# Pooled attention with a two-layer block behind it: the first batch's weight tiles are transposed on TensorE and multiplied by V in float32, and GpSimd rounds the high halves of the layer weights

## The chip, the core and the metric

The kernel runs on one core of one Trainium2 chip. The core has TensorE (PE; its weight loads are listed apart as PEld), VectorE (DVE), ScalarE (ACT), GpSimd (POOL) and SyncE (SP, which here only issues DMAs), each with its own instruction queue that runs in order. SBUF holds tiles of 128 partitions; TensorE writes to PSUM, from which ScalarE and VectorE read. The metric is the device time of one execution in microseconds (us). Every time below is from one profiled execution or from the timed runs that are named.

## The reference

Attention with pooled queries, then layer normalisation, two matrix products with a ReLU between them, and a residual:

```python
# q, k, v: (4, 8, 1152, 64) float32
q_pool = q.reshape(B, H, S // 2, 2, D).mean(axis=3)          # 576 query rows
scores = (1 / sqrt(D)) * q_pool @ k.transpose(0, 1, 3, 2)     # 576 x 1152 per head
attn = exp(scores - max(scores))
attn = attn / (sum(attn) + 1e-09)
x = attn @ v                                                 # to (4, 576, 512)
xn = (x - mean(x)) / sqrt(var(x) + 1e-06) * g_ln
out = x + relu(xn @ w_ch1) @ w_ch2                           # 512 -> 2048 -> 512
```

All inputs and the output are float32.

## The kernel before

**Precision.** Matrix products run on float16 pairs: each float32 operand is scaled by a power of two and split into a high half and a low half (what the high half left over), and three products are summed: high by high, high by low, low by high. `split_from` (L258) makes such a pair from PSUM: ScalarE writes the high half (L261), VectorE the low one (L262).

**Steps.** Two heads of one batch make a pair; there are 16 pairs of 9 steps each, 144 steps in all. A step handles one tile of 128 query rows against 1152 keys. Steps 0 to 35 are the first batch. In each pair the fifth tile (j = 4) holds the last 64 rows of both heads. `step(i)` (L850) records the work of a step in a fixed order, by hand, and each engine runs its share in that order:

- `emit_max(i)`: VectorE finds each row's maximum in PSUM (L334) and the exponent's offset (L335);
- if tile i-1 is transposed on TensorE, ScalarE and VectorE take its transpose out of PSUM (L261 and L262, tile pt);
- `emit_s(i + 1)`: nine score matmuls (L321; eighteen where j = 4) into the slot of PSUM that tile i-1 had. There are two slots, so these matmuls wait until tile i-1 has left its slot;
- `flush`: results that wait in PSUM are taken out (division by the row sums L432, L435, L439, the splits of K and Q);
- `emit_exp(i)`: ScalarE's exponential, out of PSUM into the float32 tile pe (L340);
- `a_piece`: the product of one earlier tile with V (`emit_pv`, L399);
- `some_units`: one preparation of the next pair's K or Q (six per pair, transposes L272, L275, L286) and one unit of the layer block (L520, L551), if one is ready;
- `emit_t(i)`: nine transposes of pe (L373), into the slot that the scores of tile i held;
- what was put down for this step: loads, bounds of K, Q and V by an absolute sum on ScalarE (L179), splits of V and of the layer weights.

**Two ways to transpose.** The weights of a tile must have keys on the partitions before they are multiplied by V. `on_pe` (L297) decides how. On TensorE (20 of the first batch's 36 tiles): the nine transposes, then four passes that split them out of PSUM. By DMA (the other 16, and all 108 tiles of the other batches): ScalarE writes the high half (L354), GpSimd (L238, L361) or VectorE (L363) the low half, and SP issues a DMA transpose (L366). In the first batch the low half of these is always GpSimd's. Either way `emit_pv` does 27 matmuls of 64 or 65 columns (54 half-wide ones where j = 4). The 65th column of V is one, so that it gives the row sum.

**V.** `split_v` (L240) makes V's pair on GpSimd in three passes for each head (L238 twice, L256), with a scale from the bound of V; for the first pair ScalarE and VectorE do it.

**Layer weights.** 32 blocks of 512 KB are loaded through staging buffers (L613), ScalarE takes their absolute value (L618) and VectorE rearranges their bits in three passes (L106); then 16 tiles are scaled on GpSimd (L238), rounded to the high half on ScalarE (L695), and GpSimd subtracts (L699). These are put down by step number: the blocks in steps 1 to 24 and 24 to 47, the splits after each quarter. The layer block starts at step 41, when the first batch's rows are complete. From there one of its 144 units goes with each step, and what is left runs after the last step.

## Time and profile before

| | us |
|---|---|
| three timed runs | 1001.45, 1002.28, 1005.26 (median 1002.28) |
| profiled execution | 1000.85 |
| its span, first to last instruction | 999.0 |

| engine | busy us | share of the span | instructions |
|---|---|---|---|
| PE | 841.4 | 84% | 9505 |
| PEld | 580.7 | 58% | 9505 |
| DVE | 674.9 | 68% | 1208 |
| ACT | 570.3 | 57% | 789 |
| POOL | 394.7 | 40% | 341 |

The share of an engine over the whole span is a mean over stages with different limits. The span is therefore read stage by stage: the first batch (from the first row maximum to that of step 36), the next steps, the long stretch to the last step, and the units left over. Beside the busy time stands the clock that TensorE was granted: 1.0 is 2.4 GHz, 0.5 is 1.2 GHz, and a number between is a stretch that had both.

### The profile page before, as it was taken

What the parts mean: (1) busy time and instruction counts of PE and PEld (TensorE: products, weight loads), DVE (VectorE), ACT (ScalarE), POOL (GpSimd) and SP (SyncE); (2) the same over time, 40 slices, a digit from 0 to 9 for tenths busy, and PEclk for the clock granted to TensorE, in tenths of its full rate; (3) what the DMA queues carried; (4) which work ended last, traced back from release to release, by engine and by line L of the source; (5) the groups of instructions that cost most, each with busy time, mean ns of one, the idle gap of its engine ahead of it and who ended that gap; (6) DMA issues with size and microseconds to landing.
All of it is one profiled execution on the core that took longest, in us unless ns stands there. A gap on an engine that the chain in (4) does not pass through costs nothing.

```text
span 999.0 us, 22406 instructions
## 1 busy us (share of the span) xinstructions
PE 841.4 (84%) x9505; PEld 580.7 (58%) x9505; DVE 674.9 (68%) x1208; ACT 570.3 (57%) x789; POOL 394.7 (40%) x341
## 2 busy tenths in 40 slices
PE   6565586666766679999969899999989999999998
PEld 4354464545545447666647567576656757767665
DVE  5496587867897787876777777677766777652211
ACT  3666366655655556866767577677676766521000
POOL 2253255744644455845362525344443232310000
PEclk7597676756767899999999999999998999999999
DMA  4456445463464865879787888979696867710000
GB/s 119 110 114 154 117 96 157 97 163 97 103 162 82 187 136 102 161 157 189 156 154 150 144 167 142 182 137 180 102 195 119 168 134 134 132 27 12 1 22 22
DMA packets 309044, 124.40 MB, mean 125 GB/s; under 512 B 292304, under 2 KB 292304, under 8 KB 308944
## 3 DMA queue, kind: packets, MB, share of 16 engines
q1 hardware_dynamic: 308592, 122.09, 59.8%
q8 instruction: 74, 1.21, 0.5%
q10 hardware_dynamic: 352, 0.88, 0.3%
q14 instruction: 26, 0.21, 0.1%
HBM read 45.09 MB, written 4.72 MB: 50 GB/s over the span
## 4 chain that ended last, share of the span: by engine, by line
PE 46%; DVE 29%; ACT 7%; DMA 5%; POOL 5%; issue 5%; SPq 3%; ACTq 0%; POOLq 0%; DVEq 0%
PE psum L520 15%; PE psum L551 13%; PE psum L399 7%; PE psum L321 7%; DVE mx L334 7%; DVE stage L106 4%; DVE hl L363 3%; DVE pt L262 2%; SPq L366 2%; DMA vr<-in_v_dram 2%; DVE ht L534 2%; ACT pe L340 1%; DVE wsl L106 1%; ACT kt L261 1%; DVE kt L262 1%
## 5 line engine op out<-in xcount | busy, mean ns | idle before, releaser
L321 PE MATMUL psum<-kt,qt 64*128 64x512 f16 (+3 forms) x1440 | 175.3, 363 | 63.2 <-DVE pt L262 51.5
L334 DVE TENSOR_REDUCE mx<-psum 128x1 f32<-128x1152 f32 x144 | 194.2, 1349 | 49.8 <-PE psum L399 45.7
L340 ACT ACTIVATE pe<-psum,nb,sc 128x1152 f32<-128x1152 f32 x144 | 188.7, 1310 | 25.5 <-DVE nb L335 24.6
L551 PE MATMUL psum<-wsl,ht 128*128 128x512 f16 x864 | 198.7, 383 | 2.2 <-DVE qt L262 2.0
L520 PEld LDWEIGHTS <-wsl 128*128 128x128 f16 x1920 | 174.0, 100 | 29.5 <-issue 6.2
L520 PE MATMUL psum<-xn,wsl 128*128 128x256 f16 x1536 | 183.3, 279 | 5.4 <-DVE kt L262 3.3
L399 PE MATMUL psum<-vt,pt 128*128 128x65 f16 (+3 forms) x4320 | 173.4, 201 | 0.0
L399 PEld LDWEIGHTS <-pt 128*128 128x128 f16 (+1 forms) x4320 | 157.7, 106 | 26.8 <-issue 25.2
L321 PEld LDWEIGHTS <-qt 64*128 64x128 f16 (+1 forms) x1440 | 74.0, 104 | 149.6 <-issue 115.8
L439 ACT ACTIVATE xb<-psum,r 128x64 f32<-128x64 f32 x128 | 39.9, 312 | 203.0 <-DVE r L435 196.2
L354 ACT ACTIVATE hl<-pe 128x1152 f16<-128x1152 f32 x124 | 144.3, 1164 | 13.2 <-DMA pt<-hl 9.5
L238 POOL TENSOR_SCALAR pe<-pe 128x1152 f32<-128x1152 f32 x52 | 60.7, 1168 | 208.6 <-ACT hl L354 198.3
L551 PEld LDWEIGHTS <-ht 128*128 128x128 f16 x864 | 82.4, 98 | 94.0 <-issue 6.0
L361 POOL TENSOR_TENSOR hl<-pe,hl 128x1152 f16<-128x1152 f32 x52 | 123.9, 2383 | 4.3
L363 DVE SCALAR_TENSOR_TENSOR hl<-pe,hl 128x1152 f16<-128x1152 f32 x72 | 107.9, 1498 | 0.0
L533 ACT ACTIVATE ht<-psum 128x512 f16<-128x512 f32 x72 | 42.7, 594 | 94.5 <-PE psum L520 94.2
L534 DVE SCALAR_TENSOR_TENSOR ht<-psum,ht 128x512 f16<-128x512 f32 x72 | 49.6, 689 | 69.7 <-ACT ht L533 69.0
L238 POOL TENSOR_SCALAR vt<-vr,s 128x576 f16<-128x576 f32 x30 | 23.6, 786 | 94.4 <-DVE s L231 94.4
L262 DVE SCALAR_TENSOR_TENSOR kt<-psum,s,kt 128x512 f16<-128x512 f32 (+1 forms) x48 | 31.5, 657 | 40.3 <-ACT kt L261 40.3
L161 POOL TENSOR_TENSOR qr<-qr 128x1152 f32<-128x1152 f32 (+1 forms) x8 | 21.7, 2714 | 88.1 <-DMA qr<-in_q_dram 71.0
L262 DVE SCALAR_TENSOR_TENSOR qt<-psum,s,qt 128x384 f16<-128x384 f32 x48 | 29.5, 615 | 36.4 <-ACT qt L261 36.4
L373 PE MATMUL psum<-ident,pe 128*128 128x128 f32 x180 | 33.9, 353 | 18.5 <-ACT pe L340 18.4
(104 smaller groups left out, 899.0 us busy)
## 6 DMA issues: line engine op xcount, KB each, us to landing
stage<-in_moe_w_ch_dram SPq DMA_DIRECT2D x32, 512.0 KB, 4.7
kr<-in_k_dram SPq DMA_DIRECT2D x16, 576.0 KB, 4.3
qr<-in_q_dram SPq DMA_DIRECT2D x31, 288.0 KB, 6.0
vr<-in_v_dram SPq DMA_DIRECT2D x15, 576.0 KB, 4.9
out_dram<-xb SPq DMA_DIRECT2D x32, 128.0 KB, 2.5
pt<-hl SPq DMA_TRANSPOSE x124, 4.7
vr<-in_v_dram ACTq DMA_DIRECT2D x1, 576.0 KB, 6.2
out_dram<-xh SPq DMA_DIRECT2D x4, 128.0 KB, 3.4
```

Source lines behind the costliest of these rows:

```text
L238: nc.gpsimd.tensor_scalar(dst, src, s, 1.0, op0=ALU.mult, op1=ALU.mult)
L262: lambda: nc.vector.scalar_tensor_tensor(lo, ps, s, hi, op0=ALU.mult, op1=ALU.subtract),
L321: nc.tensor.matmul(out=sp[o:o + w, c0:c0 + n], lhsT=qt[r:r + 64, qa, q0:q0 + w], rhs=kt[r:r + 64, ka, h, k0:k0 + n], start=(a == 0), stop= ...
L334: nc.vector.tensor_reduce(mx, st["s"], axis=AX.X, op=ALU.max)
L340: nc.scalar.activation(out=st["pe"], in_=st["s"], func=ACTF.Exp, scale=pair[i // C]["sc"][:, 0:1], bias=st["nb"],)
L354: nc.scalar.activation(out=hl[:, 0], in_=st["pe"], func=ACTF.Copy, scale=2.0 ** 15)
L361: nc.gpsimd.tensor_tensor(hl[:, 1], st["pe"], hl[:, 0], op=ALU.subtract)
L363: nc.vector.scalar_tensor_tensor(hl[:, 1], st["pe"], 2.0 ** 15, hl[:, 0], op0=ALU.mult, op1=ALU.subtract)
L399: nc.tensor.matmul(out=dst[:, 0:n], lhsT=lhsT, rhs=rhs, start=(u == 0 and lhsT is hi and n == 65), stop=(u == C - 1 and lhsT is lo), skip_ ...
L520: nc.tensor.matmul(out=ps[:, o:o + n], lhsT=wsl[:, 8 * w + cc, wa, f * 128:f * 128 + 128], rhs=xn[:, xa * KD + cc, 0:n], start=(m == 0), s ...
L534: lambda: nc.vector.scalar_tensor_tensor(lo, pv, 0.0, hi, op0=ALU.max, op1=ALU.subtract),
L551: nc.tensor.matmul(out=ps, lhsT=hv[0][:, ha, f, t * 128:t * 128 + 128], rhs=wsl[:, 8 * w + 4 + f // 2, wa, (f % 2) * DM:(f % 2) * DM + DM] ...
```

## The change

- All 36 tiles of the first batch go through TensorE. The transpose leaves PSUM as float32, by two copies on ScalarE; there is no high and low half, and VectorE has no part in it.
- For these tiles V stays float32: GpSimd copies each head of it into the tile that has the column of ones. The bound of V, its scale and its three passes fall away in the first four pairs, and for the first pair the two splits on ScalarE and VectorE.
- The product with V is nine float32 matmuls per tile (eighteen where j = 4) in place of 27 (54) of float16.
- GpSimd, not ScalarE, rounds the layer weights to their high half, and the three parts of a weight split come one step later, one step apart. A unit of the layer block goes out only when the splits of its weights have been put down.
- From step 36 on the tiles run as before: `low_on_pool` keeps its choice for them.

```diff
@@ split_v -> take_v
+        vt = st["v"][:, h]
+        if on_pe(p * C):
+            nc.gpsimd.tensor_copy(vt[:, :, 0:D], vr[:, h])
+            return
...
@@ on_pe
-        return 0 <= i < HP * C and (i % 2 == 0 or i % C == 4)
+        return 0 <= i < HP * C
...
@@ t_parts -> emit_t_copy
         for a, b in ((0, 512), (512, S)):
-            yield split_from(st["s"][:, a:b], 2.0 ** 15, st["pt"][:, a:b], st["pt"][:, S + a:S + b])
+            nc.scalar.copy(st["pt"][:, a:b], st["s"][:, a:b])
...
@@ emit_pv
+        if on_pe(i):
+            pt = pt.rearrange("p a n -> p (a n)").bitcast(FP32)
+            for h, q0, w, dst in parts:
+                for u, c in enumerate(ORDER):
+                    nc.tensor.matmul(
+                        out=dst, lhsT=pt[:, 128 * u + q0:128 * u + q0 + w], rhs=vt[:, h, c],
+                        start=(u == 0), stop=(u == C - 1),
+                    )
+            return ps
...
@@ w_split_b
-        nc.scalar.copy(wsl[:, n, 0], x)
+        scaled(wsl[:, n, 0], x)
...
@@ the plan of a pair, and of the weight splits
-        at(i0 + 2, bound, p, "v")
-        pre(i0 + 3, scales_reduce, p)
+        if not on_pe(p * C):
+            at(i0 + 2, bound, p, "v")
+        pre(i0 + 3, scales_reduce, p, 0, 2 if on_pe(p * C) else 3)
...
-            i0 = this[0] + 3 * n // 2
-            for x, fn in enumerate((w_split_a, w_split_b, w_split_c)):
-                at(i0 + (0, 2, 3)[x], fn, 4 * part + n)
+            i0 = this[0] + 1 + 3 * n // 2
+            for x, fn in ((0, w_split_a), (1, w_split_b), (2, w_split_c)):
+                at(i0 + x, fn, 4 * part + n)
...
@@ step
         if on_pe(i - 1):
-            parts = list(t_parts(i - 1))
-            for hi, lo in parts:
-                hi()
-            for hi, lo in parts:
-                lo()
+            emit_t_copy(i - 1)
             steps.pop(i - 1)
```

Where the order changes is seen best on three engines. On TensorE, in step 5, the product with V of an earlier tile stood in front of a K preparation (kr) and the next tile's scores (kt, qt); this is the end of its 27 matmuls, before:

```order
L399 LDWEIGHTS pt
L399 MATMUL psum<-vt,pt 128x65
L399 LDWEIGHTS pt
L399 MATMUL psum<-vt,pt 128x64
L399 LDWEIGHTS pt
L399 MATMUL psum<-vt,pt 128x65
L275 MATMUL psum<-ident,kr 64x128 x2
L321 LDWEIGHTS qt
L321 MATMUL psum<-kt,qt 128x512
```

The same place now, from the end of one step's scores to the start of the next step's:

```order
L324 LDWEIGHTS qt
L324 MATMUL psum<-kt,qt 128x128
L400 MATMUL psum<-vt,pt 128x65 x9
L278 MATMUL psum<-ident,kr 64x128 x2
L376 MATMUL psum<-ident,pe 128x128 x9
L324 LDWEIGHTS qt
L324 MATMUL psum<-kt,qt 128x512
```

The product has nine rows where it had 27 pairs, and this tile too (its number is odd) has its nine transposes between the product and the next scores.

On ScalarE, steps 7 and 8, where pe is the exponential, pt the transposed tile on its way out of PSUM, hl the high half for a DMA transpose, xb and xh results, qt a preparation; before:

```order
L261 ACTIVATE pt<-psum 128x512
L261 ACTIVATE pt<-psum 128x640
L439 ACTIVATE xh<-psum,r 64x64 x2
L261 ACTIVATE qt<-psum,s 128x384
L340 ACTIVATE pe<-psum,nb,sc 128x1152
L354 ACTIVATE hl<-pe 128x1152
L439 ACTIVATE xb<-psum,r 128x64
L261 ACTIVATE qt<-psum,s 128x384
L340 ACTIVATE pe<-psum,nb,sc 128x1152
L618 ACTIVATE wsl<-stage 128x512
```

And now:

```order
L382 COPY pt<-psum 128x512
L382 COPY pt<-psum 128x640
L453 ACTIVATE xb<-psum,r 128x64
L264 ACTIVATE qt<-psum,s 128x384
L343 ACTIVATE pe<-psum,nb,sc 128x1152
L382 COPY pt<-psum 128x512
L382 COPY pt<-psum 128x640
L453 ACTIVATE xh<-psum,r 64x64 x2
L264 ACTIVATE qt<-psum,s 128x384
L343 ACTIVATE pe<-psum,nb,sc 128x1152
```

The high half behind the exponential is gone, and two copies stand in front of every step's results and exponential.

On GpSimd, in the first quarter of the layer weights (wsl) around step 20, with the low halves of DMA tiles (pe, hl) between them; before:

```order
L238 TENSOR_SCALAR wsl<-wsl,gs_84 128x1024
L182 COPY acc<-acc 128x1
L238 TENSOR_SCALAR pe<-pe 128x1152
L361 TENSOR_TENSOR hl<-pe,hl 128x1152
L699 TENSOR_TENSOR wsl<-wsl 128x1024
L238 TENSOR_SCALAR wsl<-wsl,gs_84 128x1024
```

And now:

```order
L238 TENSOR_SCALAR wsl<-wsl,gs_84 128x1024
L182 COPY acc<-acc 128x1
L238 TENSOR_SCALAR wsl<-wsl 128x1024
L238 TENSOR_SCALAR wsl<-wsl,gs_84 128x1024
L719 TENSOR_TENSOR wsl<-wsl 128x1024
```

The low halves are gone from here, and the rounding without a scale has come in.

## Rows read from the trace of the kernel before

**Rows 1.** The page, second part: busy tenths of PE in 40 slices of the span, and the clock granted to TensorE.

```profile
PE   6565586666766679999969899999989999999998
...
PEclk7597676756767899999999999999998999999999
```

**Rows 2.** Busy time by stretch: from:to and length in us, then PE, PEld, DVE, ACT and POOL busy us with their instructions, the granted clock, the DMA share and GB/s.

```profile
21.50:264.70 243.20, 159.90 (x1744) 114.73 (x1745) 174.90 (x319) 142.61 (x208) 112.20 (x78) 0.70 0.48 118
...
393.70:861.40 467.70, 441.19 (x5474) 297.93 (x5475) 343.77 (x625) 324.23 (x432) 204.09 (x178) 0.99 0.81 153
...
327.20:393.70 66.50, 50.40 (x570) 33.74 (x569) 52.47 (x83) 38.94 (x53) 35.70 (x23) 0.90 0.66 139
```

**Rows 3.** Timeline of VectorE: the row maximum of step 0 and that of step 36 (start us, length us).

```profile
21.54 1.35 DVE L334 TENSOR_REDUCE mx<-psum 128x1 f32<-128x1152 f32 x1
...
264.75 1.36 DVE L334 TENSOR_REDUCE mx<-psum 128x1 f32<-128x1152 f32 x1 [1.46 <-PE psum L399]
```

**Rows 4.** The chain that ended last, from 21 to 265 us, by line, as a share of that stretch (the list ends where the answer cut it).

```profile
by line: DVE mx L334 9.7%; issue 9.3%; DVE pt L262 9.0%; DVE stage L106 8.6%; PE psum L321 7.8%; PE psum L399 5.7%; PE psum L373 5.3%; ACT pe L340 4.6%; DMA stage<-in_moe_w_ch_dram 4.1%; DVE wsl L106 3.2%; ACT pt L261 2.5%; DMA qr<-in_q_dra
```

**Rows 5.** Timeline of one tile transposed on TensorE, at the full clock: transposes, ScalarE's two passes, VectorE's two, and the next scores but the first.

```profile
52.70 1.20 PE L373 MATMUL psum<-ident,pe 128*128 128x128 f32 x9 [0.49 <-ACT pe L340]
53.39 1.25 ACT L261 ACTIVATE pt<-psum 128x512 f16<-128x512 f32 x2 [0.75 <-PE psum L373]
...
54.02 1.48 DVE L262 SCALAR_TENSOR_TENSOR pt<-psum,pt 128x512 f16<-128x512 f32 x2 [0.16 <-ACT pt L261]
...
55.55 0.97 PE L321 MATMUL psum<-kt,qt 64*128 64x512 f16 x8 [0.41 <-DVE pt L262]
```

**Rows 6.** The same for a tile at half the clock: transposes, ScalarE's second pass, the next scores but the first.

```profile
24.54 2.18 PE L373 MATMUL psum<-ident,pe 128*128 128x128 f32 x9 [1.71 <-ACT pe L340]
...
26.75 0.70 ACT L261 ACTIVATE pt<-psum 128x640 f16<-128x640 f32 x1 [0.47 <-PE psum L373]
...
28.37 1.75 PE L321 MATMUL psum<-kt,qt 64*128 64x512 f16 x8 [0.73 <-DVE pt L262]
```

**Rows 7.** Timeline rows of float32 work on TensorE: the one float32 product of the kernel (L203, two loads and two matmuls for each product), at the full clock and at half of it; six transposes of 64 columns (L286), at both; and the 27 float16 matmuls of one product with V at the full clock. The first two rows are from the list of line L203: shortest, median and longest in ns.

```profile
L203 PEld LDWEIGHTS psum<-dg,ones x42: 181/184/328, 11.1 to 801.5; 3*128 3x128 f32 x32, 1*128 1x128 f32 x10
L203 PE MATMUL psum<-dg,ones x42: 245/267/370, 11.1 to 801.5; 3*128 3x3 f32 x32, 1*128 1x1 f32 x10
...
50.43 0.29 PEld L203 LDWEIGHTS psum<-dg,ones 3*128 3x128 f32 x2 [1.55 <-DVE dg L198]
50.43 0.38 PE L203 MATMUL psum<-dg,ones 3*128 3x3 f32 x2 [1.22 <-DVE dg L198]
50.75 0.99 PE L399 MATMUL psum<-vt,pt 128*128 128x65 f16 x27
...
30.05 0.49 PEld L203 LDWEIGHTS psum<-dg,ones 1*128 1x128 f32 x2 [0.52 <-issue]
30.05 0.58 PE L203 MATMUL psum<-dg,ones 1*128 1x1 f32 x2
...
617.96 0.45 PEld L286 LDWEIGHTS psum<-ident,qr 64*128 64x128 f32 x6
...
13.08 0.71 PEld L286 LDWEIGHTS psum<-ident,qr 64*128 64x128 f32 x6 [0.38 <-issue]
```

**Rows 8.** Timeline around one long step: SP's DMA transpose and the load of a weight block behind it, ScalarE's wait for that block, TensorE's wait for the slot.

```profile
96.89 2.42 SPq L366 DMA_TRANSPOSE pt<-hl  x1
...
99.41 0.78 SPq L613 DMA_DIRECT2D stage<-in_moe_w_ch_dram  x1
...
103.96 0.66 ACT L618 ACTIVATE wsl<-stage 128x512 f32<-128x512 f32 x1 [5.76 <-DMA stage<-in_moe_w_ch_dram]
...
105.89 0.58 PE L321 MATMUL psum<-kt,qt 64*128 64x512 f16 x1 [5.45 <-DVE pt L262]
```

**Rows 9.** Groups of instructions from 21.5 to 264.7 us: count, then busy us and mean ns, then idle time before them and what ended it.

```profile
L361 POOL TENSOR_TENSOR hl<-pe,hl 128x1152 f16<-128x1152 f32 x15 | 35.8, 2388 | 1.2
...
L262 DVE SCALAR_TENSOR_TENSOR pt<-psum,pt 128x640 f16<-128x640 f32 x20 | 16.4, 818 | 1.4 <-ACT pt L261 1.3
...
L618 ACT ACTIVATE wsl<-stage 128x512 f32<-128x512 f32 x23 | 15.3, 667 | 9.8 <-DMA stage<-in_moe_w_ch_dram 9.8
...
L262 DVE SCALAR_TENSOR_TENSOR pt<-psum,pt 128x512 f16<-128x512 f32 x20 | 13.8, 688 | 24.9 <-ACT pt L261 24.9
...
L238 POOL TENSOR_SCALAR wsl<-wsl,wscl 128x1024 f32<-128x1024 f32 x4 | 5.2, 1298 | 0.0
```

**Rows 10.** Timeline: a GpSimd pass, a VectorE pass that falls into it, and the same VectorE pass on another block with no GpSimd pass beside it.

```profile
266.35 2.37 POOL L361 TENSOR_TENSOR hl<-pe,hl 128x1152 f16<-128x1152 f32 x1
...
267.60 1.41 DVE L106 TENSOR_SCALAR stage<-stage 128x512 int32<-128x512 int32 x1
...
292.93 0.41 DVE L106 TENSOR_SCALAR stage<-stage 128x512 int32<-128x512 int32 x1
```

**Rows 11.** The clock around a run of transposes: two stretches as in rows 2, and TensorE's timeline in the first of them.

```profile
109.50:112.90 3.40, 3.40 (x31) 3.39 (x28) 1.58 (x3) 0.60 (x1) 0.00 (x0) 0.50 0.12 49
112.90:116.40 3.50, 2.22 (x31) 1.26 (x30) 3.02 (x11) 1.02 (x3) 0.90 (x1) 0.99 0.02 5
...
110.28 1.09 PE L272 MATMUL psum<-ident,kr 128*128 128x128 f32 x4
111.16 2.02 PE L373 MATMUL psum<-ident,pe 128*128 128x128 f32 x9
```

More of the change, by code (lines that the diff above doesn't have):

```diff
@@ L238, in scaled, with take_v @@
         nc.gpsimd.tensor_scalar(dst, src, s, 1.0, op0=ALU.mult, op1=ALU.mult)
-    def split_v(p, h, fast=False):
+    def take_v(p, h):
         st = pair[p]
         vr = raws[p, "v"]
-        s = st["s"][:, 2:3]
         if "v" not in st:
             st["v"] = tr_p.tile([128, 2, C, 130], FP16, tag="v", name="vt")
-            nc.gpsimd.memset(st["v"][:, :, :, 64:66], 1.0)
+            if on_pe(p * C):
+                st["v"] = st["v"].bitcast(FP32)
+                nc.gpsimd.memset(st["v"][:, :, :, 64:65], 1.0)
+            else:
+                nc.gpsimd.memset(st["v"][:, :, :, 64:66], 1.0)
         vt = st["v"][:, h]
-        if fast:
-            hi, lo = split_from(vr[:, h], s, vt[:, :, 0:D], vt[:, :, 66:66 + D])
-            hi()
-            lo()
+        if on_pe(p * C):
+            nc.gpsimd.tensor_copy(vt[:, :, 0:D], vr[:, h])
             return
+        s = st["s"][:, 2:3]
         scaled(vt[:, :, 0:D], vr[:, h], s)
@@ L431, in one @@
         def one():
-            nc.vector.tensor_scalar(
-                r, ps[o:o + n, 64:65 * m:65], EPS, s[o:o + n], op0=ALU.add, op1=ALU.mult
-            )
+            sums = ps[o:o + n, 64:65 * m:65]
+            if on_pe(i):
+                nc.vector.tensor_scalar(r, sums, 1e-9, None, op0=ALU.add)
+            else:
+                nc.vector.tensor_scalar(r, sums, EPS, s[o:o + n], op0=ALU.add, op1=ALU.mult)
             nc.vector.reciprocal(r, r)
@@ L573, in l2 @@
             return (evac,)
-        units.extend((lambda f0=f0: l1(f0)) for f0 in range(0, 8, nf))
-        units.extend((lambda t=t, f0=f0: l2(t, f0)) for t in range(len(xs)) for f0 in (0, 4))
+        units.extend((2 * w, 4, lambda f0=f0: l1(f0)) for f0 in range(0, 8, nf))
+        units.extend(
+            (2 * w + 1, 2 + f0 // 2, lambda t=t, f0=f0: l2(t, f0))
+            for t in range(len(xs)) for f0 in (0, 4)
+        )
     def rows(b, c):
@@ L685, in w_scales @@
             )
+    w_done = [0] * 4
     def w_split_a(n):
@@ L699, in w_split_c @@
         nc.gpsimd.tensor_tensor(wsl[:, n, 1], x, wsl[:, n, 0], op=ALU.subtract)
+        w_done[n // 4] += 1
     todo = {}
@@ L837, in some_units @@
         for _ in range(1 if i < NSTEP + 5 else 2):
-            if units:
-                evacs.extend(units.popleft()())
+            if units and w_done[units[0][0]] >= units[0][1]:
+                evacs.extend(units.popleft()[2]())
     def a_piece(i):
@@ L943, in tile_pooled_attention_moe @@
         free_banks[:] = [6, 7]
-        bound(0, "v", junk=p_p.tile([128, 2, S], FP16, tag="hl", name="junk", bufs=3)[:, 0])
-        scales_reduce(0, 2, 3, lambda: [split_v(0, h, True) for h in range(2)])
+        for h in range(2):
+            take_v(0, h)
         i = 0
```

10 lines of the change are left out of this document (4 added, 6 removed).

## Prediction

> **What bounds the kernel now.** I read the slices of the page first. TensorE is six or seven tenths busy up to about 350 us and nine tenths behind it, and its clock is mixed in the first part and full in the second [rows 1]. So there are two regimes. By stretch: from 393.7 to 861.4 us PE is busy 441 of 468 us at a clock of 0.99, and this work is the same before and after. In the first batch PE is busy 160 of 243 us, DVE 175, ACT 143, at a clock of 0.70 [rows 2]. Nothing is full there; a chain binds. What the change wins or loses must come from this stretch, and since TensorE is saturated later and its later queue is unchanged, a shift of step 36 should arrive at the end nearly whole.
>
> The stretch runs from the row maximum of step 0 (21.5 us) to that of step 36 (264.75): 243.2 us, 6.76 us a step [rows 3]. Its chain names VectorE first: the row maxima 9.7%, the low halves of tiles transposed on PE (L262, pt) 9.0%, the bit passes on the layer weights (L106) 8.6 and 3.2% [rows 4]. The 9.0% are 22 us: a slot of PSUM is free for the next scores only when VectorE has written its low half behind ScalarE's high half.
>
> **The change part by part.** I build the new step from the order of TensorE's queue, which is now the same in all 36 steps: transposes, wait for the copies, next scores, product with V, preparation, transposes.
>
> *The wait for the slot.* At full clock a tile's transposes start at 52.70, ScalarE's two passes end at 54.64 (53.39 + 1.25), VectorE's end at 55.50, the scores go on at 55.55 [rows 5]. Without the low half the scores follow ScalarE: 1.94 + 0.05, so 2.0 us after the transposes start, in place of 2.85. It falls in 36 steps rather than 20, so transposing all tiles costs about what dropping the low half wins, on this path. At half the clock the second pass ends at 27.45, that is 2.91 after the start, plus the same 0.05 [rows 6].
>
> *The scores.* 0.97 us at full clock, 1.75 at half [rows 5, 6].
>
> *The product with V in float32.* The trace has no such stream, so I bound it. The one float32 product of the kernel shows two loads and two matmuls for each product, so nine products are 18 passes. From below: six transposes of 128 loaded and 64 streamed columns take 0.45 us in loads of at least 0.14 (estimated from their spacing), so 0.062 a pass at full clock, 1.1 us for 18; at half the clock six take 0.71, about 0.107 each, 1.9 us. From above: the isolated pair has its matmuls 0.38 - 0.25 = 0.13 apart at full clock, and 0.58 - 0.35 = 0.23 at half (0.35 between median and longest of that list), so 2.4 and 4.2 us [rows 7]. I take 0.08 and 0.14, nearer to the transposes, since their shape is that of this product, and the pair stands alone, so that its first load is covered by nothing: 1.44 and 2.5 us. The old product took 0.99 [rows 7]; TensorE pays more here than it did, though it has a third of the products.
>
> The Trainium skill (TensorE: Matmul & The Clock Gate, Weight-path perf modes) says that the fast weight load is off for float32, and its section on LDWEIGHTS gives 128 columns at 1.2 per ns, 107 ns. The pair's loads stand 0.29 - 0.18 = 0.11 apart, which agrees, but the transposes' loads do not. By that rule the product is 18 x 0.107 = 1.9 us; that is the third case below.
>
> *Preparation.* A pair has 28 such transposes; at 0.45 for six, 2.1 us in nine steps, 0.23 a step (0.37 at half clock) [rows 7]. For the weight sums and hand-overs between engines I allow 0.45 and 0.6, an estimate.
>
> *Sum.* Full clock: 2.0 + 0.97 + 1.44 + 0.23 + 0.45 = 5.1 us a step. Half: 2.96 + 1.75 + 2.5 + 0.37 + 0.6 = 8.2.
>
> *The clock.* In the new step TensorE works 4.1 of 5.1 us, 80%. The nearest stretch of before is 327.2 to 393.7: busy 76%, clock 0.90 [rows 2], which is a fifth of the time at the low level. I take that: 1 / (0.8/5.1 + 0.2/8.2) = 5.5 us a step, 198 us for 36.
>
> *Waits on loads.* Before, a DMA transpose kept SP's queue until GpSimd's low half was there, the load of a weight block stood behind it, and ScalarE stood 5.76 us for that block with the copies of a tile behind it; TensorE then waited 5.45 [rows 8]. In all ScalarE waited 9.8 us for blocks [rows 9], and 4.1% of the chain is such a load [rows 4]. With no DMA transpose in this stretch SP issues loads as staging buffers come free. I don't credit this again: the new sum starts from zero, and I add 14 us for what is not in it (a late Q load in front of GpSimd's pooling, the hand-overs of the scales, the start at half clock).
>
> *VectorE* loses its 40 low halves, 16.4 + 13.8 = 30.2 us [rows 9]: (174.9 - 30.2) / 36 = 4.0 us a step, below 5.1. It also loses stalls: an L106 pass takes 0.41 alone and 1.41 when a GpSimd pass of 2.37 covers it [rows 10]; 15 of those GpSimd passes go (35.8 us [rows 9]). *ScalarE* trades 16 high halves for 32 copies and is rid of the bounds of V and the seven roundings: at or below its 142.6 us, 4.0 a step, hidden under TensorE unless it waits. *GpSimd* gets 16 roundings of about 1.3 us, as its scaling of such a tile takes [rows 9]; in the first batch they are hidden, since it loses far more; from step 42 to 58 eight of them can hold up VectorE's passes, and I charge 3 us. The rounding that ScalarE drops there I credit with nothing, since TensorE sets the pace. The gate on the units holds nothing back: each quarter's splits stand before its first unit. V's copies by GpSimd are done steps before their product.
>
> Sum: 198 + 14 = 212 against 243.2, -31; with +3, -28. The profiled execution would be 1000.85 - 28 = 973 (its span and the 1.85 us around it); on the median of 1002.28, 974.
>
> **The rivals.**
>
> *More gain.* Passes at 0.062 and little low clock: 4.8 and 7.6 us a step, a tenth of the time low, 5.0 x 36 + 8 = 187: -56, 946. For it: the transposes of the same shape [rows 7]. Against it: VectorE's 4.0 and ScalarE's 4.0 a step leave little air, so some wait would show.
>
> *A small gain: float32 loads bind.* Passes at 0.109 and 0.165 (the pair's load spacing [rows 7]): 5.6 and 8.7 a step, a fifth low, 6.0 x 36 + 14 = 231: -12, 990. ScalarE as the bound, with the waits that it has now, would come out close to this.
>
> *Slower: float32 passes as slow as the isolated pair.* 0.13 and 0.23 a pass: 6.05 and 9.9 a step. The old time is 6.37 a step with the 14 us; this passes it when more than about 13% of the time is at the low clock. At 30%: 6.84 x 36 + 14 = 260: +17, 1019. For it: the first batch has 60% low clock now, and this is the only float32 product that the trace shows. Against: nothing of a stream is in that pair.
>
> *Slower: the clock stays low.* If the many transposes did not count as work, the whole batch would run at half clock: 8.2 x 36 + 14 = 309: +66, 1068. Against it: from 109.5 to 112.9 TensorE is always busy, most of it transposes from 110.28 on, and the granted clock goes from 0.50 to 0.99 right behind them [rows 11]. The Trainium skill says in the same page, under PE-mode transpose, that the full clock does not engage for transposes because they do not count as busy; by that rule this rival is the forecast. The trace does not agree.
>
> **How the numbers follow.** Forecast 0.45 (its own range 960 to 988); more gain 0.15; small gain 0.22; slow passes 0.13; low clock 0.05. The 80% range leaves out the low clock, the worse half of the slow passes and the best part of the first rival: 945 to 1011. Half a per cent, about 5 us, is what a measurement of this kernel can tell from no change: the edges of the small gain and of the slow passes meet there, 0.11. Faster 0.74, slower 0.15.
>
> **What would show it.** The row maximum of step 36 near 233 us in place of 265, and the later stretches as long as before; nine product passes of float32 in about 1.4 us at a granted clock of 0.9; TensorE's wait for the slot released by ScalarE's copy, under 1 us; no wait of ScalarE on weight blocks above 2 us. I am wrong if the float32 product takes 2 us or more at full clock, if the clock of the first batch stays near 0.7, or if step 36 comes early and the end does not follow.

## The result, and the profile after

| | us |
|---|---|
| before, on the same chip (4 runs) | 1001.87 (1000.93 to 1005.26) |
| after (4 runs) | 968.73 (962.12 to 972.16) |
| ratio | 0.9655, 95% interval 0.9593 to 0.9718 |
| profiled execution of after, and its span | 962.12, 960.3 |

The kernel became 3.5% faster; 974 was forecast, with a range of 945 to 1011. The profiled execution of after is the fastest of its four, so its trace flatters the gain a little. Medians and ratios below leave out five slow executions, each more than 1.5% above the fastest of its set (one of them took 1385 us at a granted clock of 0.55).

The page, second part, as in [rows 1]: the first quarter of PE and of its clock has risen almost throughout, the rest is much as it was.

```profile
PE   5898999887777789989788999999989999999998
...
PEclk7898999799688799999999999999999999999999
```

Busy time by stretch, columns as in [rows 2]: the first batch, the two pairs behind it, the long stretch to the last step.

```profile
21.10:224.70 203.60, 182.50 (x1548) 145.09 (x1546) 132.64 (x272) 129.56 (x205) 52.29 (x43) 0.93 0.30 98
224.70:290.60 65.90, 48.31 (x480) 36.38 (x479) 55.88 (x96) 37.40 (x52) 29.42 (x35) 0.79 0.51 122
290.60:357.40 66.80, 52.25 (x570) 34.06 (x569) 52.19 (x84) 34.88 (x49) 35.50 (x23) 0.87 0.75 139
357.40:822.90 465.50, 438.56 (x5446) 295.46 (x5445) 341.17 (x625) 320.23 (x427) 210.90 (x183) 0.99 0.81 154
```

The row maxima of step 0 and step 36, as in [rows 3]:

```profile
21.15 1.35 DVE L337 TENSOR_REDUCE mx<-psum 128x1 f32<-128x1152 f32 x1
...
224.67 1.36 DVE L337 TENSOR_REDUCE mx<-psum 128x1 f32<-128x1152 f32 x1
```

The whole gain lies where it was looked for. The first batch takes 203.6 us in place of 243.2, VectorE works 133 us in it and not 175, TensorE 182.5 and not 160, and the clock is 0.93 and not 0.70. Step 36 comes 40 us earlier, and the span ends 38.7 us earlier (960.3 against 999.0).

The chain that ended last, 21 to 225 us, by line, as in [rows 4]:

```profile
by line: PE psum L400 29.4%; ACT pt L382 16.5%; PE psum L324 14.7%; PE psum L376 8.0%; DMA stage<-in_moe_w_ch_dram 7.2%; DMA qr<-in_q_dram 3.0%; PE psum L289 2.5%; SPq L128 1.9%; ACT pe L343 1.8%; issue 1.8%; PE psum L663 1.7%; PE psum L275
```

VectorE led this chain before, in four of its lines; now it is not among those shown. The float32 product (L400), ScalarE's copies (L382), the scores (L324) and the transposes (L376) fill 69% of it: it is TensorE's queue, with the copies as the one gap in it. One step at the full clock shows that, in the manner of [rows 5]: transposes, ScalarE's copies, the next scores but the first, and the product with V (its loads, its matmuls).

```profile
48.89 1.15 PE L376 MATMUL psum<-ident,pe 128*128 128x128 f32 x9
49.53 1.24 ACT L382 COPY pt<-psum 128x512 f32<-128x512 f32 x2 [0.41 <-PE psum L376]
...
50.82 0.97 PE L324 MATMUL psum<-kt,qt 64*128 64x512 f16 x8 [0.28 <-ACT pt L382]
...
51.98 2.09 PEld L400 LDWEIGHTS psum<-vt,pt 128*128 128x128 f32 x18
52.01 2.20 PE L400 MATMUL psum<-vt,pt 128*128 128x65 f32 x18
```

And the longest step, at half the clock, in the manner of [rows 6, 8]: ScalarE stands 1.75 us for a weight block with the copies of a tile behind it, TensorE waits for them, the clock of this stretch is 0.50, and the product takes 4.10 us.

```profile
182.32 0.66 ACT L636 ACTIVATE wsl<-stage 128x512 f32<-128x512 f32 x1 [1.75 <-DMA stage<-in_moe_w_ch_dram]
182.89 1.16 ACT L382 COPY pt<-psum 128x512 f32<-128x512 f32 x2
183.51 2.35 PE L324 MATMUL psum<-kt,qt 64*128 64x512 f16 x9 [1.85 <-ACT pt L382]
...
185.79 4.10 PE L400 MATMUL psum<-vt,pt 128*128 128x65 f32 x18
```

The stretch of that step, columns as in [rows 2]:

```profile
179.70:190.00 10.30, 8.44 (x39) 6.60 (x38) 4.20 (x10) 6.97 (x12) 7.06 (x6) 0.50 0.71 263
```

Last the waits in the first batch (engine, tile, line, what it waited for: us in all, times, the longest). Of the kernel before, the wait for a slot:

```profile
PE psum L321 <- DVE pt L262: 51.5, 34, 6.4
```

Of the kernel after, the same wait, and that of ScalarE for a weight block:

```profile
PE psum L324 <- ACT pt L382: 13.8, 36, 2.1
...
ACT wsl L636 <- DMA stage<-in_moe_w_ch_dram: 1.8, 1, 1.8
```

TensorE's wait for a slot fell by 37.7 us, which is nearly the 39.6 by which the batch got shorter. That is an agreement of two numbers and no proof: the wait may have been filled by other things. The runs below ask.

### The profile page after: what moved, and what is told of

It reads as the page before. It is cut to its first block, busy times and chain, and to the rows that moved or that the text cites. A ratio compares the mean times of both kernels' runs of the same rounds, so it can differ in the third digit from the quotient of the medians.

```text
span 960.3 us, 21835 instructions
## 1 busy us (share of the span) xinstructions
PE 867.4 (90%) x9286; PEld 613.8 (64%) x9286; DVE 630.6 (66%) x1160; ACT 549.5 (57%) x779; POOL 343.4 (36%) x315
## 4 chain that ended last, share of the span: by engine, by line
PE 55%; DVE 22%; ACT 9%; DMA 7%; issue 3%; SPq 3%; POOL 1%; ACTq 0%; DVEq 0%; POOLq 0%
PE psum L534 14%; PE psum L565 14%; PE psum L324 8%; PE psum L400 7%; PE psum L411 6%; DVE mx L337 5%; ACT pt L382 4%; DVE hl L366 3%; DMA pt<-hl 3%; DVE stage L106 3%; PE psum L289 2%; PE psum L376 2%; DVE ht L548 2%; DMA stage<-in_moe_w_ch_dram 2%; SPq L128 1%
## 5 line engine op out<-in xcount | busy, mean ns | idle before, releaser
L324 PE MATMUL psum<-kt,qt 64*128 64x512 f16 (+3 forms) x1440 | 165.1, 339 | 25.8 <-ACT pt L382 14.1
L324 PEld LDWEIGHTS <-qt 64*128 64x128 f16 (+1 forms) x1440 | 70.6, 99 | 110.8 <-issue 72.6
L453 ACT ACTIVATE xb<-psum,r 128x64 f32<-128x64 f32 x128 | 40.1, 313 | 170.6 <-DVE r L449 165.0
L357 ACT ACTIVATE hl<-pe 128x1152 f16<-128x1152 f32 x108 | 125.7, 1164 | 14.7 <-DMA pt<-hl 11.5
L411 PEld LDWEIGHTS <-pt 128*128 128x128 f16 (+1 forms) x3240 | 108.4, 101 | 21.0 <-issue 20.5
L411 PE MATMUL psum<-vt,pt 128*128 128x65 f16 (+1 forms) x3240 | 119.9, 195 | 0.0
L366 DVE SCALAR_TENSOR_TENSOR hl<-pe,hl 128x1152 f16<-128x1152 f32 x72 | 103.8, 1441 | 0.0
L238 POOL TENSOR_SCALAR pe<-pe 128x1152 f32<-128x1152 f32 x36 | 42.3, 1176 | 152.8 <-ACT hl L357 142.5
L364 POOL TENSOR_TENSOR hl<-pe,hl 128x1152 f16<-128x1152 f32 x36 | 85.4, 2373 | 3.0
L400 PE MATMUL psum<-vt,pt 128*128 128x65 f32 (+1 forms) x720 | 85.0, 276 | 0.0
L400 PEld LDWEIGHTS psum<-vt,pt 128*128 128x128 f32 (+1 forms) x720 | 81.0, 191 | 3.5 <-issue 3.4
L382 ACT COPY pt<-psum 128x512 f32<-128x512 f32 x72 | 44.5, 638 | 47.2 <-PE psum L376 47.2
L265 DVE SCALAR_TENSOR_TENSOR kt<-psum,s,kt 128x512 f16<-128x512 f32 (+1 forms) x48 | 31.5, 658 | 39.6 <-ACT kt L264 38.6
```

The costliest lines, as they stand in the source:

```text
L324: nc.tensor.matmul(out=sp[o:o + w, c0:c0 + n], lhsT=qt[r:r + 64, qa, q0:q0 + w], rhs=kt[r:r + 64, ka, h, k0:k0 + n], start=(a == 0), stop= ...
L357: nc.scalar.activation(out=hl[:, 0], in_=st["pe"], func=ACTF.Copy, scale=2.0 ** 15)
L364: nc.gpsimd.tensor_tensor(hl[:, 1], st["pe"], hl[:, 0], op=ALU.subtract)
L366: nc.vector.scalar_tensor_tensor(hl[:, 1], st["pe"], 2.0 ** 15, hl[:, 0], op0=ALU.mult, op1=ALU.subtract)
L382: nc.scalar.copy(st["pt"][:, a:b], st["s"][:, a:b])
L400: nc.tensor.matmul(out=dst, lhsT=pt[:, 128 * u + q0:128 * u + q0 + w], rhs=vt[:, h, c], start=(u == 0), stop=(u == C - 1),)
```

## The experiments

Theory A, from the prediction: in the first batch TensorE's own queue sets the step, and what counts is what stands in it, the wait for the slot and the price of the product. Its rival B takes another form in each run, and mostly says that the gain came from elsewhere or that another engine binds at once. Twelve runs were made, on several chips; where two kernels are compared below that ran on different chips, it is by their ratios (1% is 10 us). "The batch" is from the row maximum of step 0 to that of step 36 in the profile; the ratio is to the kernel before on the same chip.

| run | median us | ratio, 95% | batch us | its clock |
|---|---|---|---|---|
| before | 1001.87 | 1 | 243.2 | 0.70 |
| after | 968.73 | 0.9655 (0.9593 to 0.9718) | 203.6 | 0.93 |
| before without the low half | 969.59 | 0.9716 (0.9674 to 0.9757) | 210.2 | 0.75 |
| before, all 36 tiles on TensorE | 1010.69 | 1.0115 (1.010 to 1.013) | 254.6 | 0.77 |
| after, low half put back | 1070.85 | 1.0697 (1.063 to 1.0764) | 318.2 | 0.61 |
| after, product done twice | 1032.78 | 1.0322 (1.0273 to 1.037) | 267.1 | 0.95 |
| after, product at its old price | 942.48 | 0.9434 (0.9405 to 0.9463) | 187.9 | 0.89 |
| before, weight blocks a step later | 989.48 | 0.9894 (0.9851 to 0.9937) | 234.6 | 0.70 |
| after, weight blocks a step later | 972.11 | 0.9687 (0.9628 to 0.9747) | 217.7 | 0.85 |
| after, rounding back on ScalarE | 972.13 | 0.973 (0.9701 to 0.9759) | 217.6 | 0.87 |
| after, product ahead of the scores | 1080.45 | 1.0828 (1.0803 to 1.0853) | 310.8 | 0.68 |
| after, product in the gap | 948.35 | 0.9476 (0.9436 to 0.9516) | 191.0 | 0.90 |
| the same, weight blocks a step later | 948.29 | 0.949 (0.9464 to 0.9517) | 190.4 | 0.88 |

The batch and the clock are of one profiled execution each. The product in the gap has a second set of times below, and its batch and clock are from a profile of that set.

**The kernel before without VectorE's low half.** VectorE's pass is taken away from the 20 tiles on TensorE, and with it its wait; the product uses the high half in its place. The other 16 tiles still go by DMA.

```diff
-            for hi, lo in parts:
-                lo()
             steps.pop(i - 1)
@@ emit_pv
                 hi, lo = pt[:, u, q0:q0 + w], pt[:, C + u, q0:q0 + w]
+                if on_pe(i):
+                    lo = hi
```

> The kernel before, without VectorE's low half of the 20 tiles that are transposed on TensorE in the first batch; their product with V uses the high half in its place, so that TensorE's 27 matmuls stay (the low part of these weights is left out of the computation). Everything else of the change is left off: the other 16 tiles go by DMA transpose, V is split, ScalarE rounds the layer weights. Theory A (the wait for the slot is the largest part of the gain): 20 tiles by 0.85 us is -17 us directly, and the clock rises from 0.70, which gives as much again: -17 to -32 us, 968 to 983. Rival B (the steps of the 16 tiles that go by DMA, and the loads behind them, set the pace of the batch, so that a shorter step on TensorE only waits longer in the next one): 0 to -8 us, 992 to 1000.

969.59 us, at the better end of A's range. The batch in the profile, columns as in [rows 2]:

```profile
21.20:231.40 210.20, 149.49 (x1747) 107.52 (x1746) 153.03 (x279) 140.49 (x207) 113.82 (x78) 0.75 0.56 137
```

The wait for the slot in it:

```profile
PE psum L321 <- ACT pt L261: 22.1, 21, 5.8
```

Twenty low halves fewer (30.2 us of VectorE's work [rows 9]) make the batch 33.0 us shorter; TensorE's wait for a slot falls from 51.5 to 22.1. By its time this kernel cannot be told from the whole change: the ratios are 0.9716 and 0.9655, and the intervals overlap. So everything else in the change, taken together, brought some 6 us or nothing; these runs do not settle which. The run does not separate VectorE's shorter queue from the earlier release; the waits speak for the release.

**The kernel before with all 36 tiles on TensorE,** still split, with the old product. (The first tile of the third group of four weight tiles isn't scaled here, since its turn had passed when it was put down; one GpSimd pass is left out.)

```diff
-        return 0 <= i < HP * C and (i % 2 == 0 or i % C == 4)
+        return 0 <= i < HP * C
```

> The kernel before with all 36 tiles of the first batch transposed on TensorE, but still split into float16 halves by ScalarE and VectorE and multiplied in 27 matmuls: one part of the change alone. Theory A (the float32 path counts because it takes VectorE's low half out of the step; the new product itself costs TensorE more): TensorE's loop is 2.85 + 0.97 + 1.0 + 0.4 = 5.2 us as in the changed kernel, but VectorE needs 4.0 + 1.5 = 5.5 us a step and waits besides, so step 36 comes at 235 to 250 us against 225, and the time is 978 to 992. Rival B (the gain comes from the DMA transposes and GpSimd's low halves that are gone; the split is harmless): within 4 us of the changed kernel, 965 to 973.

1010.69 us: slower than before by 11 us, where both theories gave a gain; B falls, and so does A's time. With no DMA transpose and no GpSimd low half left in the batch, the wait for VectorE is longer than before, in all tiles:

```profile
PE psum L321 <- DVE pt L262: 63.4, 66, 5.1
```

**The kernel after with the low half put back,** as a pass on VectorE that nothing reads.

```diff
         for a, b in ((0, 512), (512, S)):
             nc.scalar.copy(st["pt"][:, a:b], st["s"][:, a:b])
+        for a, b in ((0, 512), (512, S)):
+            nc.vector.scalar_tensor_tensor(
+                spare[:, a:b], st["s"][:, a:b], 1.0, st["pt"][:, a:b], op0=ALU.mult, op1=ALU.subtract
+            )
```

> The kernel after, with one thing put back: behind ScalarE's two copies of a transposed tile VectorE again writes a low half from PSUM (of the same two shapes as before, into a spare tile that nothing reads), so that a slot is free for the next scores only behind VectorE. The output is the same. Theory A (the slot's release is in the path of every step, because TensorE's next scores wait for it): each of 36 steps gets longer by what the low half took behind the copy, 2.85 - 2.0 = 0.85 us, so +31 us, 995 to 1002, row maximum of step 36 near 255, and TensorE's wait for the slot is released by VectorE. Rival B (the gain came from the loads, the clock and the freed GpSimd; the order of ScalarE and VectorE behind the transposes matters little): less than +10 us, 968 to 978.

1070.85 us, by the ratios 104 us more than after. A's sign, three times its size. The timeline of a step shows A's mechanism (transposes, copies, VectorE, scores, product):

```profile
92.50 1.15 PE L376 MATMUL psum<-ident,pe 128*128 128x128 f32 x9
...
93.13 1.24 ACT L383 COPY pt<-psum 128x512 f32<-128x512 f32 x2 [1.22 <-PE psum L376]
...
93.78 1.45 DVE L385 SCALAR_TENSOR_TENSOR spare<-psum,pt 128x512 f16<-128x512 f32 x2
...
95.28 0.97 PE L324 MATMUL psum<-kt,qt 64*128 64x512 f16 x8 [0.39 <-DVE spare L385]
...
96.18 2.22 PE L405 MATMUL psum<-vt,pt 128*128 128x65 f32 x18
```

The stretches show where the rest is: the whole batch, four steps, and a single step, columns as in [rows 2].

```profile
22.60:340.80 318.20, 271.43 (x1544) 216.18 (x1545) 176.18 (x341) 132.43 (x206) 50.88 (x43) 0.61 0.19 62
44.90:85.40 40.50, 36.27 (x185) 28.55 (x184) 20.70 (x43) 13.66 (x21) 0.00 (x0) 0.50 0.05 14
92.30:98.40 6.10, 4.83 (x41) 3.85 (x40) 3.88 (x7) 3.89 (x6) 0.00 (x0) 1.00 0.35 99
```

From transposes to scores 2.78 us, against 1.93 in after: the 0.85 of theory A. The step that has the full clock takes 6.2 us (the same step of after 5.3). But most steps do not have it: the four take 10.1 us each at half the clock, and the batch has 0.61. 36 x 0.85 = 31 us of the 115 by which the batch grew are the wait; the other 84 came with the lower clock. This was not in A. Why the clock stays low is not shown: in the four steps TensorE is recorded busy for 36.3 of 40.5 us.

**The product done twice,** and **the product at its old price.** The first repeats each float32 product; in the second the copies and V are float16 and there are 27 matmuls on high halves, as many as before.

```diff
-            for h, q0, w, dst in parts:
+            for h, q0, w, dst in [x for x in parts for _ in range(2)]:
```

> The changed kernel with each float32 product done twice (the second overwrites the first with the same sums). Theory A (TensorE's queue is the loop of a step, so each product pass is paid in full): 18 more passes of 0.115 us, 2.07 us a step, 74 us in all: 1040 to 1046, and step 36 at 295 to 305. Rival B (ScalarE's loop of copies, exponential and results, about 4.2 us, or VectorE's binds and the product is partly covered): 40 us or less on top, 1000 to 1010.

```diff
                 for u, c in enumerate(ORDER):
-                    nc.tensor.matmul(
-                        out=dst, lhsT=pt[:, 128 * u + q0:128 * u + q0 + w], rhs=vt[:, h, c],
-                        start=(u == 0), stop=(u == C - 1),
-                    )
+                    for x, n in enumerate((65, 64, 65)):
+                        nc.tensor.matmul(
+                            out=dst[:, 0:n], lhsT=pt[:, u, q0:q0 + w], rhs=vt[:, h, c, 0:n],
...
```

> The kernel after, with TensorE's price of the product alone put back to that of before: ScalarE's copies of a transposed tile write float16, GpSimd's copy of V writes float16, and the product is 27 matmuls of 65, 64 and 65 columns as before, each on the high halves (the low halves of the weights and of V are left out of the computation). The float32 product took 2.20 us, this one should take 0.99. Theory A (TensorE's queue binds in each step): 36 steps by 1.2 us, -43 us, 922 to 932, step 36 near 183. Rival B (below a step of some 4.8 us the row maximum, the exponential and the copies on VectorE and ScalarE, and the loads, bind): -10 to -25 us, 944 to 959, with TensorE's waits in the first batch above 40 us.

Twice: 1032.78, and the batch grew by 63.5 us, 1.8 a step: a little less than A gave, and far from B. At the old price: 942.48, by the ratios 22 us less than after. That is B's size, half of A's; but B's sign, waits of TensorE above 40 us in the batch, did not come (it is idle for 33.8 of 187.9 us). Where no load is late and the clock is 1.00, steps 5 to 10, the comparison is clean. The stretch in after, columns as in [rows 2]:

```profile
43.60:76.60 33.00, 30.55 (x280) 24.65 (x279) 21.57 (x48) 22.62 (x37) 0.00 (x0) 1.00 0.24 63
```

The same six steps with the old price:

```profile
42.50:69.90 27.40, 24.31 (x342) 18.06 (x341) 21.45 (x47) 21.79 (x37) 0.00 (x0) 1.00 0.24 63
```

Six steps take 5.6 us less, 0.93 each, of the 1.2 that the product lost (2.20 to 0.97). So in these steps TensorE's queue binds to about three quarters, and over the batch the rest meets the next chain: the transposes now wait for the exponential, 12.4 us in all (3.1 in after).

```profile
PE psum L375 <- ACT pe L342: 12.4, 13, 2.3
```

The batch of the profiled execution got 15.7 us shorter, not 33: two steps of 9.8 and 9.4 us remain in it, the clock is 0.89 and not 0.93, and the two profiles are of the fastest execution of after and the slowest of this kernel.

**Weight blocks a step later,** on the kernel before and on the kernel after.

```diff
-        at(i0 + 1, w_bias, m)
+        at(i0 + 2, w_bias, m)
```

> The kernel before, with ScalarE's pass on each layer-weight block (w_bias) one step later and nothing else. It measures what the waits behind loads cost the kernel before, where DMA transposes hold the queue that issues the loads; the change did away with these in the first batch. Theory A (ScalarE's 9.8 us of waiting for blocks delay the copies of a tile, and through them TensorE, and the clock falls behind each): -8 to -15 us, 985 to 992, so that a quarter to a half of the change's gain is this. Rival B (the waiting is hidden, and the gain is the shorter path through PSUM): within 3 us of the kernel before.

> The kernel after, with ScalarE's pass on each layer-weight block (w_bias) one step later, so that its load has one step more to arrive. Theory A (the long steps 12 to 14 and 29 come of ScalarE standing for a block with the copies of a tile behind it, after which the clock falls): step 29 goes from 10.25 to below 7 us, in all -5 to -12 us, 957 to 964. Rival B (those steps are late for the Q load and its pooling on GpSimd, or the clock falls anyway): within 3 us of the kernel after, 966 to 972.

Before: 989.48, -10.6 us, as A said, though the clock of the batch stays at 0.70. ScalarE's wait for blocks in the batch is gone (9.8 us in [rows 9]), and TensorE's wait for a slot falls from 51.5 to 40.8 us:

```profile
L618 ACT ACTIVATE wsl<-stage 128x512 f32<-128x512 f32 x22 | 14.6, 665 | 0.0
```

So some 10 us, a third of what the change gained, was to be had by one number in the plan. After: 972.11, not told from the kernel after; B holds. The long step 29 did go from 10.26 to 6.13 us, but other steps became long in this execution, and the batch has a lower clock, not a higher one:

```profile
21.60:239.30 217.70, 199.64 (x1547) 158.34 (x1546) 130.27 (x272) 129.92 (x205) 51.82 (x43) 0.85 0.28 91
```

**The rounding of the weights back on ScalarE,** in the kernel after.

```diff
-        scaled(wsl[:, n, 0], x)
+        nc.scalar.copy(wsl[:, n, 0], x)
```

> The changed kernel with the high halves of the layer weights rounded on ScalarE again. Theory A (this part is hidden, since TensorE sets the pace): within 4 us of the changed kernel, 965 to 973. Rival B (ScalarE's 16 passes of 1.04 us stand in the loop of copies and exponentials): 8 to 16 us slower than it. Rival C (GpSimd's rounding holds VectorE up): 3 to 8 us faster than it, all of it between steps 36 and 58.

972.13, by the ratios 7 us above the kernel after, and the two intervals overlap: between A's 4 us and B's 8, not settled. C falls. In the profiled execution the batch is 14.0 us longer than that of after. The place is steps 30 to 35, where ScalarE's rounding (L715) waits for GpSimd and the copies of a tile stand behind it:

```profile
213.16 2.12 POOL L719 TENSOR_TENSOR wsl<-wsl 128x1024 f16<-128x1024 f32 x1
...
215.31 1.05 ACT L715 CAST wsl<-wsl 128x1024 f16<-128x1024 f32 x1 [2.05 <-POOL wsl L719]
...
216.26 1.17 ACT L382 COPY pt<-psum 128x512 f32<-128x512 f32 x2
...
216.89 2.35 PE L324 MATMUL psum<-kt,qt 64*128 64x512 f16 x9 [1.96 <-ACT pt L382]
```

From 191.4 to 238.8 us the clock is 0.67 in this execution. In after the same steps, 190.0 to 224.7, have 0.96. So whether moving the rounding helps is not shown. If it does, then by these rows less for the passes that ScalarE is rid of than because ScalarE no longer waits for GpSimd ahead of a copy; that wait comes once in this batch.

**The product ahead of the scores.** After shows TensorE idle while ScalarE copies. Two kernels try to put the product there; the first leaves it in the slot's own bank, the second takes a bank outside the slots and evacuates it behind the exponential.

```diff
+        if live and on_pe(i - 1):
+            kept, evacs[:] = list(evacs), []
+            a_piece(i)
+            late, evacs[:] = list(evacs), kept
         if i + 1 < NSTEP:
             emit_s(i + 1)
...
+            evacs.extend(late)
```

> The changed kernel with the product with V put on TensorE's queue ahead of the next scores in the first batch, so that it covers the wait for the copies out of the slot. Theory A (that wait, about 0.8 us in 36 steps, stands bare on TensorE's queue and nothing else is near): 20 to 30 us faster than the changed kernel, 939 to 949, step 36 at 195 to 205. Rival B (the exponential, behind the copies and results on ScalarE, is next and takes most of the room): 0 to 8 us faster.

1080.45: both theories failed. The bank belongs to the slot whose row maximum VectorE is still reading, so the product can stand waiting for it, and the scores behind it come late. A step of TensorE's timeline:

```profile
145.32 4.10 PE L400 MATMUL psum<-vt,pt 128*128 128x65 f32 x18 [1.75 <-DVE mx L337]
...
149.35 1.78 PE L324 MATMUL psum<-kt,qt 64*128 64x512 f16 x9
```

TensorE's waits from 21 to 350 us, those of the transposes and of the product:

```profile
PE psum L376 <- ACT pe L343: 55.5, 33, 3.0
...
PE psum L400 <- DVE mx L337: 9.8, 9, 2.3
```

The product waits for the row maximum in nine steps only. Most of TensorE's waiting is that of the transposes for the exponential, as rival B's chain would have it. That all of it comes of the bank is argued and not shown: the next kernel changes the bank and also the place where the product is taken out.

```diff
+        if on_pe(i) and i > 2:
+            pieces.extend(ready.pop(i, ()))
+            n = pieces.popleft()
+            ps = emit_pv(n, bank())
+            late = [*evac_pv(n, ps), lambda n=n: evacuated(n)]
         if i + 1 < NSTEP:
             emit_s(i + 1)
...
             emit_exp(i)
+            for fn in late or ():
+                fn()
```

> The kernel after, with the product with V of the first batch recorded ahead of the next scores, in one of the two banks outside the slots (6 or 7), and its evacuation recorded behind the exponential. TensorE can then work on the product while ScalarE copies the transposed tile out; in the run with the product first in the slot's own bank the row maximum stood in its way, here nothing does. Theory A (TensorE's own queue binds, with about 0.75 us of each step spent waiting for the copies): that wait goes in 33 steps, -20 to -27 us, 941 to 949, step 36 near 200, TensorE's waits for pt below 10 us in all in the first batch. Rival B (behind the wait another chain is as long: row maximum, exponential, copies on VectorE and ScalarE): -8 to +3 us, 960 to 972, and TensorE waits as long in front of its transposes instead.

948.35: in A's range, though by the ratios it is 18 us less than after, and A gave 20 to 27. A second set of times, with the profile that is read here:

> The kernel with the product in the gap once more, for a profile taken at the clock of its timed runs. Both theories as before: A: row maximum of step 36 near 200, TensorE's wait for the copies below 10 us in all in the first batch; B: step 36 near 205 to 215, with the wait moved in front of the transposes. Its time 945 to 952.

952.50 and 963.86, ratio 0.9586 (0.9511 to 0.9661): the two sets together reach from 946.79 to 963.86, a wider spread than that of after, and this second set alone cannot be told from after. The timeline of one step of the 952.50:

```profile
47.92 1.15 PE L376 MATMUL psum<-ident,pe 128*128 128x128 f32 x9
...
48.74 1.17 ACT L382 COPY pt<-psum 128x512 f32<-128x512 f32 x2
...
48.91 2.12 PE L400 MATMUL psum<-vt,pt 128*128 128x65 f32 x18
...
50.96 0.99 PE L324 MATMUL psum<-kt,qt 64*128 64x512 f16 x9
```

Steps 5 to 10 of it, columns as in [rows 2]:

```profile
43.40:70.30 26.90, 26.90 (x276) 23.71 (x276) 21.26 (x48) 21.96 (x36) 0.00 (x0) 1.00 0.24 67
```

The product now starts while ScalarE copies, the scores wait for nothing, and in steps 5 to 10 TensorE is never idle: 26.9 us in place of 33.0. (Its busy time falls too, from 30.55 to 26.90; 2.1 us of that are the scores, whose first matmul no longer stands alone ahead of the wait.) In the whole batch the wait for the copies is 7.9 us, below A's 10:

```profile
PE psum L324 <- ACT pt L382: 7.9, 8, 2.9
```

The transposes wait 5.5 us for the exponential, so B's wait did not move there. But step 36 came at 213.8, as B said, and not near 200: steps 11 to 14 and 29 to 33 have up to 8.3 us, with ScalarE waiting 7.8 us in two waits for weight blocks.

> The kernel with the product in the gap, and ScalarE's pass on each layer-weight block one step later. In the profile of the product in the gap two waits of ScalarE for blocks (3.9 and 4.0 us) stand in steps 25 and 29, and from the second on the clock is 0.73 and steps 29 to 33 take 7.4 to 8.3 us in place of some 4.7. Theory A (with the queue of TensorE shorter, the blocks come too late, and a step more removes the wait and the low clock behind it): -8 to -16 us against the 949 of the product in the gap, 933 to 941. Rival B (as with the same edit on the kernel after, another stall lets the clock fall elsewhere): within 4 us, 945 to 953.

948.29: B. The two steps named became short (4.81 and 4.08 us), and others long (11.50 and 8.99). This kernel is faster than after by about 16 us; that of the product in the gap is so by its first set of times, and by its second not clearly.

## Why the prediction was right, and where it was not

**Place and sign.** Right. The stretch, the shift of step 36, and that it arrives at the end nearly whole: 40.1 us at step 36 and 38.7 at the end of the profiled execution, against 31 and 28 forecast. By the medians the gain is 33 us.

**The wait for the slot.** Right in size: 2.0 us forecast from [rows 5], 1.93 measured, released by ScalarE's copy. Wrong in the remark that transposing all tiles costs about what dropping the low half wins: all tiles alone cost 11 us and the low half alone brought 31. The effects also do not add: with all tiles on TensorE, from the split and the old product to the kernel after, it is some 46 us by the ratios.

**The scores.** 0.97 us, as forecast.

**The product: the step that failed.** "I take 0.08 and 0.14" per pass. Measured are 2.20 us for 18 passes at the full clock and 4.10 at half, so 0.122 and 0.228. The loads alone take 2.09 us, 0.116 each, nearly the whole time of the product. The bounds from [rows 7] held it (0.062 to 0.13), but the choice did not: the isolated pair was the near row, not the six transposes. The forecast dismissed it because its first load is covered by nothing. In the stream each load costs as much. Nor was it right that the trace had no such stream: nine float32 transposes of 128 x 128 took 1.20 and 2.18 us, 0.133 and 0.242 a pass [rows 5, 6], close to the product's 0.122 and 0.228. Their loads, of the same size as the product's, took 0.108 each:

```profile
52.70 0.97 PEld L373 LDWEIGHTS psum<-ident,pe 128*128 128x128 f32 x9 [0.73 <-ACT pe L340]
```

The six transposes that the forecast went by have loads of 64 rows and not 128; no run shows whether that makes them cheaper. The Trainium skill (TensorE: Matmul & The Clock Gate, its section on LDWEIGHTS) gives columns / 1.2 ns for a load, 107 ns for 128 columns, and says under Weight-path perf modes that the fast load is off for float32. The trace agrees within a tenth at the full clock (0.116 us); at half the clock it is 0.217 us (3.91 for 18).

**Why the time came out all the same.** By my own formula, with only the product's price put right, the step would be 5.86 us (9.8 at half clock), the batch 36 x 6.37 + 14 = 243, and the forecast no change. Four terms were too large and made up for it:

- preparation and allowance, 0.68 us at full clock: steps 5 to 10 take 33.0 / 6 = 5.5 us, which leaves 0.4 beside 1.93 + 0.97 + 2.20. With 5.5 and some 9.4 at half clock (an estimate: 2.96 + 1.75 + 4.10 and the allowance of 0.6), 14 us less;
- low clock for a fifth of the time: it was (1 - 0.93) / 0.5 = 14%, 6 us less;
- the 14 us for what is not in the sum: left out here, on the argument that late loads show as steps at the low clock, which the sum has already;
- 36 steps: the first takes 1.5 us, before as after, so 35 count, 4 us less.

243 - 14 - 6 - 14 - 4 = 205 or so, and 203.6 were measured. This sum is made after the fact; no run measures its terms one by one. By it the structure of the forecast was right, the price of the product was a third too low, and the allowances hid it. "I am wrong if the float32 product takes 2 us or more at full clock" came true, while the time held. That is luck as to size.

**VectorE and ScalarE.** Hidden for the most part, as forecast: 133 and 130 us in 203.6. ScalarE is at the edge: its copies are 16.5% of the chain, and at the old price of the product TensorE begins to wait for its exponential.

**Loads.** ScalarE's wait for blocks fell from 9.8 to 1.8 us, its longest 1.75, below the 2 us named. The run on the kernel before puts the worth of that wait at about 11 us there.

**GpSimd.** The 3 us charged behind the batch: steps 36 to 143 take 598.2 us, against 596.7 before and 596.1 with the rounding on ScalarE. Right in size. The moved rounding, which was credited with nothing, is worth some 7 us by the run that puts it back, and that is not clear of the noise.

**The rivals.** "A small gain" had a price nearer than the forecast's (0.109 and 0.165 a pass against 0.122 and 0.228 measured) and a time of 990, because it kept the other terms. "Slow passes" had the nearest price of all (0.13 and 0.23); it came out slower than before because it kept them too and put 30% of the time at the low clock, where 14% was measured. "The clock stays low" fell: with 315 recorded transposes of 128 x 128 in the batch the granted clock is 0.93. The Trainium skill (TensorE: Matmul & The Clock Gate, Part 4: PE-mode transpose) says that the full clock does not engage for transposes. This trace does not agree in so far as nine of them take 1.15 us at a granted clock of 1.00, against 2.18 at half of it [rows 6]. Whether they hold the clock up by themselves the batch cannot show, since they are about a fifth of a step (1.15 of 5.5 us); the one stretch that is mostly transposes [rows 11] speaks for it.

**What stays open.** Which part of the 33 us without the low half is the earlier release and which VectorE's shorter queue; and what decides, from execution to execution, in which steps of the batch the clock falls.

## What to carry to other kernels

Look for what holds a double buffer the longest: here leaving out one pass of VectorE, which held a slot for 0.85 us behind ScalarE's, took 31 us off the kernel, about as much as the whole change (33 us); how much of that is the slot and how much VectorE's shorter queue is open. Before moving work to a costlier type on the engine that will bind, price it by all rows of that type, the dear ones too, and not by the cheapest of a like shape, and don't let allowances stand in for a measurement. Once the chain is one engine's queue, try to put its longest independent piece into its remaining gap, in a bank that nothing else is using; here that brought 7 to 18 us.

## What the runs showed of the hardware

- A float32 matmul of 128 x 128 by 65 columns is recorded as two loads and two matmuls, and costs 0.24 us in a stream at the full clock, 0.46 at half; three float16 ones of the old product cost 0.11 (0.99 us for 27). So here float32 was dearer than the three float16 products that it replaces.
- A stall cost more than its length. A pass that adds 0.85 us to a step at the clock of 1.00, so 31 us to 36 steps, added 115 us to the batch: the clock of the batch went from 0.93 to 0.61, and a step at half clock took 10.1 us and not 6.2.
- The reverse did not hold: taking one wait away (the blocks a step later, in after) shortened that step by 4 us, but the kernel not measurably (972.11 against 968.73); the clock fell in other steps.
